# Last batch of a channel mixer: 15 block products in place of 18, the first third ahead of the batch before

## The chip, the cores and the metric

The kernel runs on one core of one Trainium2 chip. The metric is the time of one execution on the device, in microseconds (us), as the median of several runs; beside it stands a profile of one execution. TensorE (PE in the profile) multiplies matrices into PSUM, VectorE (DVE) and ScalarE (ACT) do elementwise work, GpSimd (POOL) a little at the start, and SyncE (SP) issues the DMAs. Each engine works off its own queue in order and waits for the others at semaphores.

## The reference

For 4 batches of 8 heads, 768 positions and a head size of 48, an attention with a gated outer-product state is followed by a mixer of width 8 x 48 = 384. All data are float32.

```python
f = 1.0 / (1.0 + np.exp(-f_logit))
for t in range(S):
    state = f[:, :, t, :, None] * state + np.einsum('bhd,bhe->bhde', k[:, :, t], v[:, :, t])
    y[:, :, t] = np.einsum('bhd,bhde->bhe', q[:, :, t], state)
x = np.ascontiguousarray(y.transpose(0, 2, 1, 3)).reshape(B, S, H * D)

xt = x.transpose(0, 2, 1)
h = xt @ U @ V                       # rank 32, over the positions
u = x + h.transpose(0, 2, 1)
ch = np.maximum(u @ w_ch1, 0.0) @ w_ch2      # 384 -> 1536 -> 384
return (u + ch).astype(np.float32)
```

The two big products are `u @ w_ch1` (the first layer) and the product with `w_ch2` (the second layer).

## The kernel before

`factored_path` does all the work here. Attention goes through 16 units of two heads each (4 units a batch), in chunks of 64 positions. `steps` lists a unit's pieces: `scores` (sc, L587), `kept` (pt, L608), `read` and `inner` (y, L662 and L680), `states` (ds, L624), `scan`, and of the next units `gates`, `keep`, `keys`, `read_back` and `queries`, which use VectorE's 32x32 transposes (L481) and scans (L538, L556, L645) on the tiles fz, kz, qT, X, Y, fT and added. The last piece, `inner`, copies y into the batch's x (L686, ACT).

The class `Mixer` makes the pieces of one batch's mixer. A batch has 768 positions, worked in three thirds of 256 tokens (`a` = 0, 1, 2). `before` holds `low_rank` (ph, L144), `added_up` (a second ph, L152), `mix` (pu, L169, added into x by VectorE) and per third a `turn` (put, L179): six 128x128 transposes of x on TensorE, copied to uT by ACT (L180). The first layer of a third is six pieces of `ch1` (pz, L191), each of six matmuls with 128x128 weights from w1 and 256 columns of uT. Each fills a PSUM bank, and ACT applies the relu on its way to z (L198). An f32 matmul leaves two records in the profile, each with its own weight load (PEld).

The second layer of batches 1 to 3 already uses a scheme of seven products. `sums_of` makes four sums of z on VectorE (S, held in w_raw tiles, 128x768), `quarters` has made sums of w2 beforehand, and `seven` does four steps with 12, 12, 12 and 6 matmuls of 192 columns (pw, L236), each followed by small adds on VectorE and a copy on ACT (L249). All adds of the mixer go through one helper, L159, which gives them a high priority. Steps 2 and 3 store the two output tiles. Batch 0 uses the plain second layer (po, L213).

The order on TensorE is written out by hand. `self.main` lists the first-layer pieces of a third among the second-layer steps of the one before, and `after` is the second layer of the last third. While attention works on batch b + 1, the class `Fill` deals out the mixer pieces of batch b between attention's pieces, each with a cost and when its share is due; `attention` puts out what is left at the end. Then `start_mixer` puts the pieces of `before` among those of `after`. After the last batch's attention nothing is left to go beside: its `main` and `after` stand alone, behind a check of the gates' smallest product (low, lp, lowest, ok). The order of the VectorE and ACT queues behind the first batch comes from a scheduler, by dependencies and priorities; in-order queues then keep it.

PSUM has two pools: `ps_big`, three tiles of two banks each (put, pu, sc, pt, ds, y), and `ps_mm`, two tiles of one bank (ph, pz, pw, po). A matmul that takes a tile waits until its last reader is done.

Of the kernel before, what the change touches and what calls it, by code (L numbers as in the profile page):

```python
# [10 lines left out]
F32 = mybir.dt.float32  # L11
U32 = mybir.dt.uint32
U64 = mybir.dt.uint64
I32 = mybir.dt.int32
AF = mybir.ActivationFunctionType
ALU = mybir.AluOpType
AX = mybir.AxisListType

WP = 384

RAW = 4
# [6 lines left out]

SMALLEST = struct.unpack("f", struct.pack("I", 896 << 20))[0]
LARGEST = struct.unpack("f", struct.pack("I", (1151 << 20) - 2))[0]  # L30


def weight_loader(nc, pool, dma):
# [53 lines left out]
class Fill:  # L87


    def __init__(self, pieces, portions):  # L90
        self.pieces = list(pieces)
        self.share = sum(c for c, _ in self.pieces) / portions
        self.due = 0.0
# [27 lines left out]
class Mixer:  # L121
# [2 lines left out]

    def __init__(self, tc, b, x, U, V, w1, w2, sums, ident, blocks, out, two, three, zp, ps_big, ps_mm, wide=False):
        nc = tc.nc
        P = nc.NUM_PARTITIONS
        NCH, DM = x.shape[1], x.shape[2]  # L130
        R, FF = U.shape[2], w1.shape[2]
        NG = P // R
        NDC, NFC = DM // P, FF // P
# [22 lines left out]
        def add(*args):  # L156

            with tc.high_priority(offset=AHEAD):
                nc.vector.tensor_tensor(*args)  # L159
# [25 lines left out]
        def ch1(a, j):  # L185

            pm = ps_mm.tile([P, 512], F32, name="pz", tag="mm")
            for i in range(2):
                for m in range(NDC):
                    o = (2 * j + i) * P  # L190
                    nc.tensor.matmul(pm[:, i * 2 * P : (i + 1) * 2 * P], lhsT=w1[:, m, o : o + P],  # L191
                                     rhs=uT[a][:, m, :], start=(m == 0), stop=(m == NDC - 1))
            c, k = divmod(2 * j, NI)
            if k == 0:

                own = wide and c == 1
                z[a, c] = zp.tile([P, NI, 2 * P], F32, name="zw" if own else "z")
            nc.scalar.activation(z[a, c][:, k : k + 2, :].rearrange("p i t -> p (i t)"), pm, AF.Relu)  # L198

        def store(t, o):  # L200
            nc.sync.dma_start(out=out[b, t * P : (t + 1) * P, :], in_=o)
# [18 lines left out]
        def part(a, r, c):  # L220
            return z[a, c][:, :, r * P : (r + 1) * P]

        def sums_of(a):
            for i in range(1, 5):
                s = two.tile([P, WP], U64, name="w_raw", bufs=RAW)
                S[i] = s.bitcast(F32).rearrange("p (i t) -> p i t", t=P)
            add(S[1], part(a, 1, 0), part(a, 1, 1), ALU.add)
            add(S[2], S[1], part(a, 0, 0), ALU.subtract)
            add(S[3], part(a, 0, 0), part(a, 1, 0), ALU.subtract)
            add(S[4], part(a, 0, 1), S[2], ALU.subtract)  # L230

        def products(a, *of):
            pm = ps_mm.tile([P, 512], F32, name="pw", tag="mm")
            for n, (lhs, rhs) in enumerate(of):
                for i in range(NI):
                    nc.tensor.matmul(pm[:, n * HM : (n + 1) * HM], lhsT=lhs[:, i, :], rhs=rhs[:, i, :],  # L236
                                     start=(i == 0), stop=(i == NI - 1))
            return pm
# [4 lines left out]
        def seven(a, step):  # L243
            x0, x1 = x[:, 2 * a, :], x[:, 2 * a + 1, :]
            if step == 0:
                pm = products(a, (part(a, 0, 0), w2[:, 0:NI, lo]), (part(a, 0, 1), w2[:, NI:NFC, lo]))
                s = W["s"] = two.tile([P, WP], U32, name="w_y").bitcast(F32)
                o = W["o0"] = three.tile([P, DM], F32, name="o")
                nc.scalar.copy(s[:, hi], pm[:, lo])  # L249
                add(s[:, lo], x0[:, lo], pm[:, lo], ALU.add)  # L250
                add(o[:, lo], s[:, lo], pm[:, hi], ALU.add)
            elif step == 1:
                pm = products(a, (S[2], sums[2]), (S[3], sums[3]))
                s, o = W["s"], W["o0"]
                add(s[:, hi], s[:, hi], pm[:, lo], ALU.add)
                add(o[:, hi], s[:, hi], pm[:, hi], ALU.add)
                o1 = W["o1"] = three.tile([P, DM], F32, name="o")
                add(o1.rearrange("p (n d) -> p n d", n=2), x1.rearrange("p (n d) -> p n d", n=2),
                    o[:, hi].unsqueeze(1).broadcast_to((P, 2, HM)), ALU.add)
                add(s[:, hi], s[:, hi], x0[:, hi], ALU.add)  # L260
            elif step == 2:
                pm = products(a, (part(a, 1, 1), sums[4]), (S[1], sums[1]))
                add(W["o1"], W["o1"], pm[:, 0:DM], ALU.add)
                store(2 * a + 1, W["o1"])
                add(W["s"][:, hi], W["s"][:, hi], pm[:, hi], ALU.add)
            else:
                pm = products(a, (S[4], w2[:, NI:NFC, hi]))
                add(W["o0"][:, hi], W["s"][:, hi], pm[:, lo], ALU.add)
                store(2 * a, W["o0"])

        def second(a):
            if sums is None:
# [21 lines left out]
            self.main += ready(a) + ahead[: NI // 2] + second(a) + ahead[NI // 2 :]  # L294
        self.main += ready(NA - 1)
        self.after = second(NA - 1)


def quarters(nc, pool, w2):
# [22 lines left out]
def factored_path(ctx, tc, q, k, v, f_logit, moe_U, moe_V, moe_w_ch1, moe_w_ch2, out, ok):  # L322
# [22 lines left out]

    TURNED = HP + HP // 2

    assert S % (2 * P) == 0 and H % 2 == 0 and NB < D <= PAD and PAD == 2 * NB and S % NB == 0 and W == NBL * 2 * PAD
    assert DM % P == 0 and FF % P == 0 and FF % WP == 0 and DM == WP and DM <= 512 and R % 32 == 0 and P % R == 0 and P // R <= NBL and NFC % 4 == 0 and NBL == 6
    assert NBL * PAD <= 512 and C == PAD  # L350
# [8 lines left out]

    raw = [{nm: const.tile([P, W], F32, name=f"{nm}_raw{i}") for nm in "fkq"} for i in range(2)]
    nat = [
        {nm: t.rearrange("p (c h d) -> p c h d", h=2, d=PAD) for nm, t in slot.items()}
        for slot in raw
# [54 lines left out]
    for s in range(2):  # L420
        half = causal[s * C : (s + 1) * C, :]
        nc.gpsimd.affine_select(out=half, in_=half, compare_op=ALU.is_ge, fill=0.0, base=0,
                                pattern=[[1, C]], channel_multiplier=-1)
    ends = const.tile([P, S], F32, name="ends")
    nc.vector.memset(ends, 0.0)
    nc.vector.memset(ends.rearrange("p (c t) -> p c t", t=C)[:, :, C - 1], 1.0)
    starts = const.tile([P, S], F32, name="starts")
    nc.gpsimd.memset(starts, 0.0)

    fz = [const.tile([P, S + 1], F32, name=f"fz{i}") for i in range(2)]  # L430
# [56 lines left out]
    def prepare(n):  # L487
# [33 lines left out]
        def gates():  # L521
            f0 = T["f0"] = two.tile([P, NCH], F32, name="f0")
            if n < TURNED:
                pt = on_tensor("f")
                nc.scalar.activation(halves(f)[:, :, :, 1:C], pt[:, :, :, 1:C], AF.Sigmoid)
                nc.scalar.activation(f0.rearrange("p (a c) -> p a c", a=2), pt[:, :, :, 0], AF.Sigmoid)
                follow("f")
                return
            fT = one.tile([P, S], F32, name="fT")
            turned(fT, r["f"])  # L530
            follow("f")
            fv = fT.rearrange("p (c t) -> p c t", t=C)
            nc.scalar.activation(by_chunk[:, :, 1:C], fv[:, :, 1:C], AF.Sigmoid)  # L533
            nc.scalar.activation(f0, fv[:, :, 0], AF.Sigmoid)

        def keep():
            X = T["X"] = one.tile([P, S], F32, name="X")
            nc.vector.tensor_tensor_scan(  # L538
                backwards(X, S - 1, S), backwards(f, S, S), backwards(ends, S - 1, S), 0.0,
                ALU.mult, ALU.add,  # L540
            )
            X0 = X.rearrange("p (c t) -> p c t", t=C)[:, :, 0]
            nc.scalar.copy(least[:, n, :], X0)
            X1 = two.tile([P, NCH], F32, name="X1")
            nc.vector.tensor_single_scalar(X1, X0, LEAST, ALU.max)
            nc.vector.reciprocal(starts.rearrange("p (c t) -> p c t", t=C)[:, :, 0], X1)
            whole = wholes[n % 2]
            nc.vector.tensor_tensor(whole[:, 1:NCH], T["f0"][:, 1:NCH], X0[:, 1:NCH], ALU.mult)
# [3 lines left out]
            follow("k")  # L552

        def read():
            Y = T["Y"] = one.tile([P, S], F32, name="Y")
            nc.vector.tensor_tensor_scan(Y, f[:, 0:S], starts, 0.0, ALU.mult, ALU.add)  # L556

        def queries():
# [5 lines left out]
    x_tiles = {}  # L564

    def mixer(b):
        return Mixer(tc, b, x_tiles[b], U, V, w1, w2, sums if b else None, ident, blocks, out, two, three, zp, ps_big, ps_mm, b == 0)

    def attend(n):

# [150 lines left out]
            if n + 2 < NU:  # L721
                load(n + 2, "v")

    def attention(pieces, portions, todo):

        fill = Fill(todo, portions)
        for piece in pieces:
            fill()
            piece()
        fill.rest()  # L730

    def start_mixer(b, after):

# [69 lines left out]
            f()  # L803
    for b in range(2, B):
        todo, after = m.main, m.after
        attention(steps(b * HP + 1, (b + 1) * HP + 1), 10 * HP, todo)
        m = start_mixer(b, after)
    todo, after = m.main, m.after

    low = one.tile([P, 1], F32, name="low")  # L810
# [338 lines left out]
```

## Time and profile before

| what | us |
|---|---|
| median of 9 runs | 500.92 (499.68 to 501.49) |
| the profiled execution's own time | 500.32 |
| its span, first to last instruction | 498.6 |
| TensorE matmuls busy | 483.1 |
| VectorE busy | 278.4 |
| ScalarE busy | 157.7 |
| first layer's matmuls (L191), all batches | 196.0 |
| second layer by seven products (L236), all its groups | 131.6 |
| last `inner` of attention ends | 363.6 |
| last batch's transposes (put) | 403.3 to 405.3 |
| last batch's first and second layer | 405.4 to 493.0 |

A line of the costliest groups or of the table by shape gives the line of the kernel, engine, operation, output and inputs, shapes and count, then the busy time and the mean of one in ns, then the idle time in front of it. A line of the timeline gives the start, the time from the first to the last of a run of equal instructions, and what they are. Matmuls are pipelined, so the duration of one record is longer than the spacing of two. The chain of waits follows the end back from what released what, and gives for each piece the start and the time it adds.

### The profile page before, as it was taken

What the parts mean: (1) busy time and instruction counts of PE and PEld (TensorE: products, weight loads), DVE (VectorE), ACT (ScalarE), POOL (GpSimd) and SP (SyncE); (2) the same over time, 40 slices, a digit from 0 to 9 for tenths busy, and PEclk for the clock granted to TensorE, in tenths of its full rate; (3) what the DMA queues carried; (4) which work ended last, traced back from release to release, by engine and by line L of the source; (5) the groups of instructions that cost most, each with busy time, mean ns of one, the idle gap of its engine ahead of it and who ended that gap; (6) DMA issues with size and microseconds to landing.
All of it is one profiled execution on the core that took longest, in us unless ns stands there. A gap on an engine that the chain in (4) does not pass through costs nothing.

```text
span 498.6 us, 11989 instructions
## 1 busy us (share of the span) xinstructions
PE 483.1 (97%) x5279; PEld 401.6 (81%) x5279; DVE 278.4 (56%) x402; ACT 157.7 (32%) x297; POOL 36.3 (7%) x49
## 2 busy tenths in 40 slices
PE   7997999999999999999999999999999999999995
PEld 4775688886666578898898788898899888999995
DVE  4896789778998487666665436632411431122232
ACT  2434576564434123423323122313311122101010
POOL 3001345441000000000000000000000000000000
PEclk9998999999999999999999999999999999999998
DMA  9989956784777323406234100100000000000001
GB/s 146 153 180 164 285 147 156 163 139 55 113 114 123 69 41 49 63 12 115 38 49 82 24 33 1 26 1 33 3 1 34 0 35 0 1 32 1 32 2 37
DMA packets 158676, 34.30 MB, mean 69 GB/s; under 512 B 149206, under 2 KB 157078, under 8 KB 158614
## 3 DMA queue, kind: packets, MB, share of 16 engines
q1 hardware_dynamic: 158614, 33.44, 36.5%
q8 instruction: 43, 0.70, 0.6%
q14 instruction: 19, 0.16, 0.1%
HBM read 28.70 MB, written 4.72 MB: 67 GB/s over the span
## 4 chain that ended last, share of the span: by engine, by line
PE 93%; DMA 2%; DVE 1%; issue 1%; ACT 1%; SPq 0%; DVEq 0%; ACTq 0%
PE pz L191 39%; PE pw L236 24%; PE po L213 10%; PE y L662 3%; PE y L680 3%; PE ds L624 3%; PE sc L587 3%; PE pt L504 2%; PE idle L752 2%; PE put L179 2%; PE pt L608 2%; PE ph L144 1%; PE pu L169 1%; DMA f_raw<-in_f_logit_dram 1%; DMA k_raw<-in_k_dram 1%
## 5 line engine op out<-in xcount | busy, mean ns | idle before, releaser
L191 PE MATMUL pz<-uT,w 128*128 128x256 f32 x864 | 196.0, 382 | 0.1
L191 PEld LDWEIGHTS pz<-uT,w 128*128 128x128 f32 x864 | 161.0, 190 | 22.4 <-issue 0.3
L198 ACT ACTIVATE z<-pz 128x512 f32<-128x512 f32 x63 | 37.5, 596 | 129.9 <-PE pz L191 125.8
L236 PE MATMUL pw<-w,z 128*128 128x192 f32 x324 | 56.5, 329 | 0.4 <-DVE o L159 0.4
L236 PE MATMUL pw<-zw,w_raw 128*128 128x192 f32 x324 | 55.9, 327 | 0.8 <-DVE o L159 0.8
L236 PEld LDWEIGHTS pw<-zw,w_raw 128*128 128x128 f32 x324 | 53.0, 190 | 2.2 <-DVE o L159 2.1
L236 PEld LDWEIGHTS pw<-w,z 128*128 128x128 f32 x324 | 52.8, 190 | 2.3 <-DVE o L159 1.6
L159 DVE TENSOR_TENSOR w_raw<-z 128x768 f32<-128x768 f32 x18 | 17.2, 954 | 56.3 <-ACT z L198 56.3
L538 DVE TENSOR_TENSOR_SCAN X<-fz,ends 128x768 f32<-128x768 f32 x16 | 28.1, 1756 | 9.9 <-ACT fz L533 5.1
L69 POOL TENSOR_TENSOR w<-w_y,w_r 128x384 int32<-128x384 int32 x24 | 30.2, 1257 | 36.5 <-DVE w_y L68 30.8
L556 DVE TENSOR_TENSOR_SCAN Y<-fz,starts 128x768 f32<-128x768 f32 x16 | 27.9, 1745 | 0.2
L213 PE MATMUL po<-w,zw 128*128 128x384 f32 x72 | 25.6, 499 | 0.0
L213 PE MATMUL po<-w,z 128*128 128x384 f32 x72 | 25.3, 496 | 0.0
L594 DVE TENSOR_TENSOR A<-sc,causal 128x768 f32<-128x768 f32 x16 | 15.2, 948 | 16.9 <-PE sc L587 16.9
L159 DVE TENSOR_TENSOR w_y<-x,pw 128x192 f32<-128x192 f32 x9 | 3.2, 354 | 38.2 <-ACT w_y L249 38.2
L650 ACT COPY st<-added 128x576 f32<-128x576 f32 x12 | 14.6, 1220 | 23.7 <-DVE added L645 23.7
L159 DVE TENSOR_TENSOR w_y<-w_y,pw 128x192 f32<-128x192 f32 x18 | 6.3, 349 | 25.5 <-PE pw L236 25.5
L213 PEld LDWEIGHTS po<-w,zw 128*128 128x128 f32 x72 | 12.9, 189 | 8.7 <-issue 1.2
L213 PEld LDWEIGHTS po<-w,z 128*128 128x128 f32 x72 | 13.1, 190 | 8.5 <-DVE o L159 0.6
L680 PEld LDWEIGHTS y<-v_nat,A 64*64 64x64 f32 x768 | 13.5, 139 | 7.7 <-issue 6.3
L236 PE MATMUL pw<-w,w_raw 128*128 128x192 f32 x108 | 19.2, 328 | 0.0
L66 DVE TENSOR_SCALAR w_y<-w_y 128x384 f32<-128x384 f32 (+3 forms) x27 | 11.8, 438 | 12.3 <-ACT w_y L64 12.1
(101 smaller groups left out, 531.9 us busy)
## 6 DMA issues: line engine op xcount, KB each, us to landing
w_raw<-in_moe_w_ch_dram SPq DMA_DIRECT2D x18, 384.0 KB, 3.9
out_dram<-o SPq DMA_DIRECT2D x24, 192.0 KB, 1.9
v_nat<-in_v_dram SPq DMA_DIRECT2D x16, 144.0 KB, 3.0
v_nat<-in_v_dram SPq DMA_DIRECT2D x32, 72.0 KB, 2.9
zw<-in_moe_w_ch_dram SPq DMA_DIRECT2D x6, 384.0 KB, 5.6
f_raw<-in_f_logit_dram SPq DMA_DIRECT2D x20, 96.0 KB, 3.1
k_raw<-in_k_dram SPq DMA_DIRECT2D x20, 96.0 KB, 2.6
q_raw<-in_q_dram SPq DMA_DIRECT2D x20, 96.0 KB, 2.7
```

Source lines behind the costliest of these rows:

```text
L69: nc.gpsimd.tensor_tensor(dst.bitcast(I32), shaped(y.bitcast(I32)), shaped(r), ALU.add)
L159: nc.vector.tensor_tensor(*args)
L191: nc.tensor.matmul(pm[:, i * 2 * P : (i + 1) * 2 * P], lhsT=w1[:, m, o : o + P], rhs=uT[a][:, m, :], start=(m == 0), stop=(m == NDC - 1))
L198: nc.scalar.activation(z[a, c][:, k : k + 2, :].rearrange("p i t -> p (i t)"), pm, AF.Relu)
L213: nc.tensor.matmul(pm, lhsT=z[a, i // NI][:, i % NI, s * P : (s + 1) * P], rhs=w2[:, i, :], start=(i == 0), stop=(i == NFC - 1))
L236: nc.tensor.matmul(pm[:, n * HM : (n + 1) * HM], lhsT=lhs[:, i, :], rhs=rhs[:, i, :], start=(i == 0), stop=(i == NI - 1))
L538: nc.vector.tensor_tensor_scan(backwards(X, S - 1, S), backwards(f, S, S), backwards(ends, S - 1, S), 0.0, ALU.mult, ALU.add,)
L556: nc.vector.tensor_tensor_scan(Y, f[:, 0:S], starts, 0.0, ALU.mult, ALU.add)
L587: nc.tensor.matmul(sc[part[s ^ par], par, c * C : (c + 1) * C], lhsT=T["k"][rows[par], chunk[2 * c + s]], rhs=T["q"][rows[par], chunk[2 * ...
L594: nc.vector.tensor_tensor(T["A"], sc[:, :, 0 : NBL * C].rearrange("p h (c i) -> p h c i", i=C), causal.unsqueeze(1).unsqueeze(1).broadcast ...
L624: nc.tensor.matmul(ds[par * PAD : (par + 1) * PAD, s, c * D : (c + 1) * D], lhsT=T["kb"][part[s ^ par], par, i, :], rhs=vt[part[s ^ par], ...
L680: nc.tensor.matmul(o(s, par, c), lhsT=T["A"][part[s ^ par], par, c, :], rhs=vt[part[s ^ par], c, par, :], start=False, stop=True, skip_gro ...
```

## The change

The first layer of the last batch is done by another scheme. A third of 256 tokens times w1 is a product of a 2 x 3 grid of blocks (128 tokens x 128 channels) with a 3 x 3 grid (128 channels x 512). Plainly that is 18 products of blocks. The scheme takes 15 products, of sums of blocks of x (`X_SUMS`, 10 sums of 128x128 a third) with sums of blocks of w1 (`W_SUMS`, 14 sums of 128x512, made once). The results (`VALUES`) are put together from the products: per third two copies on ACT and 19 sums of 128x512 on VectorE, then six relus on ACT, in place in z.

A product is four matmuls of 128x128 weights and 128 columns, with the block of w1 as weights. Two products share a tile of `ps_big` (`two_of`), so a third has eight pieces (seven pairs and a single one), and the sums follow as soon as their products are there.

The order changes too. In the last attention round, what `Fill` has not dealt out is kept back. `sum_of_w` is called beside the pieces of the second half of that round. Then the last batch's `low_rank`, `added_up` and `mix` come first, each followed by one of the kept pieces; the transposes and two rounds of sums of x follow; and the first third's pieces (`early`) are put among the rest of batch 2's mixer. The check of the gates comes after that, then thirds 1 and 2, each among the second-layer steps of the third before.

Room is found in tiles that are free by then. The raw f, k and q of one slot, ends, X, Y and fT become parts of one tile `late`, the other slot and starts parts of `other`, and z becomes `z_all`. The sums of w1 go over `late`, fz and added, the sums of x over v_nat and st, the values over kz, A and qT, z of thirds 0 and 2 over `other`, and the four sums S of third 1 over blocks of w1 that no product uses any more. The products of the last third's second layer take a tile of `ps_big`.

```diff
+X_SUMS = (
+    (7, 3, '+', 5), (6, 2, '+', 5), (11, 3, '+', 6), (13, 0, '+', 11), (8, 4, '-', 6), (9, 1, '+', 8),
+    (10, 2, '+', 8), (12, 9, '-', 0), (15, 10, '-', 12), (14, 3, '-', 12),
+)
...
+PRODUCTS = (
+    ((2, 17),), ((7, 18),), ((11, 20),), ((6, 21),), ((13, 0),), ((1, 3),), ((8, 15),), ((4, 19),),
+    ((9, 10),), ((10, 16),), ((3, 22),), ((12, 11),), ((0, 12),), ((15, 13),), ((14, 9),),
+)
+VALUES = (
+    (13, 'p0', None, None), (15, 'p1', None, None), (14, 'v15', '+', 'p2'), (12, 'v14', '-', 'p3'), (6, 'p4', '-', 'v14'),
+    (0, 'v6', '-', 'v13'), (0, 'v0', '+', 'p5'), (11, 'v12', '+', 'v13'), (11, 'p6', '-', 'v11'), (3, 'p7', '-', 'v11'),
...
         def products(a, *of):
-            pm = ps_mm.tile([P, 512], F32, name="pw", tag="mm")
+            if room and a == NA - 1:
+                pm = ps_big.tile([P, 2, 512], F32, name="pw", tag="big")[:, 0]
+            else:
+                pm = ps_mm.tile([P, 512], F32, name="pw", tag="mm")
...
+            def settle():
+                while todo:
+                    n, p, sign, q = todo[0]
+                    if any(o is not None and got(o) is None for o in (p, q)):
+                        return
...
+                    if q is None:
+                        nc.scalar.copy(dst, left)
+                    else:
+                        combine(dst, left, sign, right)
...
+                    if n < 6 and not any(v[0] == n for v in todo):
+                        nc.scalar.activation(dst, dst, AF.Relu, scale=float(SIGNS[n]))
+
+            def two_of(k):
+                pm = ps_big.tile([P, 2, 512], F32, name="pp", tag="big")
+                for i, of in enumerate(PRODUCTS[k : k + 2]):
+                    for r in range(FG):
+                        for xn, wn in of:
+                            nc.tensor.matmul(
+                                pm[:, i, r * P : (r + 1) * P], lhsT=room["w"](wn)[:, r * P : (r + 1) * P],
+                                rhs=x_node(a, xn), start=((xn, wn) == of[0]), stop=((xn, wn) == of[-1]),
+                            )
+                    have[k + i] = pm[:, i, 0 : FG * P].rearrange("p (i t) -> p i t", t=P)
+                settle()
...
+        if room:
...
+            i = len(self.before) - NA + 1
+            self.before[i:i] = more(0)
+            self.before[i + 2 : i + 2] = more(1)
+            self.early = fewer(0)
+            self.main = []
+            for a in range(NA - 1):
+                f, s = fewer(a + 1), second(a)
+                self.main += ready(a) + f[:4] + (more(a + 2) if a == 0 else []) + f[4:5]
+                if a < NA - 2:
+                    self.main += s[:1] + f[5:6] + s[1:2] + f[6:7] + s[2:3] + f[7:] + s[3:]
+                else:
+                    self.main += f[5:6] + s[:1] + f[6:] + s[1:2] + ready(NA - 1) + s[2:]
...
         todo, after = m.main, m.after
-        attention(steps(b * HP + 1, (b + 1) * HP + 1), 10 * HP, todo)
-        m = start_mixer(b, after)
+        pieces = steps(b * HP + 1, (b + 1) * HP + 1)
+        if b == B - 1:
+            pieces = beside(pieces, 10 * (HP - 2), [lambda i=i: sum_of_w(i) for i in range(len(W_SUMS))])
+        rest = attention(pieces, 10 * HP, todo, b < B - 1)
+        if b < B - 1:
+            m = start_mixer(b, after)
+
+    m, rest = mixer(B - 1), rest + after
+    pieces = [p for pair in zip(m.before[:3], rest) for p in pair] + m.before[3:]
+    rest = rest[3:]
+    for i, piece in enumerate(m.early):
+        n = -(-len(rest) // (len(m.early) - i))
+        pieces += [piece] + rest[:n]
+        rest = rest[n:]
+    for _, piece in pieces:
+        piece()
     todo, after = m.main, m.after
```

## The prediction

> **What bounds the kernel now.** I read the busy times first, then the chain that ended last, then the stretches around the change, then single instructions.
>
> The page says that TensorE's matmuls are busy almost always, and VectorE (DVE) about half the time:
>
> ```profile
> PE 483.1 (97%) x5279; PEld 401.6 (81%) x5279; DVE 278.4 (56%) x402; ACT 157.7 (32%) x297; POOL 36.3 (7%) x49
> ```
>
> The chain of waits from the last attention matmul to the end, in order of time (start, us, what), is matmuls with almost no holes:
>
> ```profile
> 363.00 0.64 PE y L680 x44
> 363.64 13.85 PE pw L236 x84
> ...
> 385.26 3.90 PE pw L236 x24
> 389.16 1.41 PE ph L144 x12
> ...
> 403.31 1.97 PE put L179 x18
> 405.27 0.11 PE lp L813
> 405.38 23.31 PE pz L191 x108
> 428.69 13.65 PE pw L236 x84
> 442.35 15.54 PE pz L191 x72
> ```
>
> So in this part a microsecond off TensorE is a microsecond off the kernel, as long as nothing else becomes late. The busy times of three stretches (columns: stretch, length, then busy time per engine) tell how much room VectorE has:
>
> ```profile
> 320.00:340.00 20.00, 20.00 (x268) 18.77 (x268) 9.15 (x15) 4.83 (x8) 0.00 (x0) 1.00 0.05 14
> 340.00:363.60 23.60, 23.60 (x457) 19.59 (x449) 6.91 (x8) 7.75 (x13) 0.00 (x0) 1.00 0.03 11
> 405.10:493.00 87.90, 87.86 (x471) 81.97 (x468) 21.20 (x41) 12.81 (x23) 0.00 (x0) 1.00 0.04 12
> ```
>
> In the last 88 us VectorE works 21 us. The granted clock is 1.00 in all three.
>
> **Part 1: fewer products on TensorE.** Each f32 matmul leaves two records. From the chain: 128x256 takes 23.31 / 108 = 0.2158 us a record (L191), 128x192 takes 13.65 / 84 = 0.1625 (L236). The slope between them is 0.0533 / 64 = 0.833 ns a column, so 128 columns should take 0.1625 - 64 x 0.000833 = 0.109 us, if the weight load does not become the limit. That is the one unknown that decides the sign: the new matmuls have half the columns, and each still loads its own 128x128 weights. Transposes of 128 columns do run at 1.97 / 18 = 0.109, but their weight loads last 140 ns in the table by shape, those of f32 matmuls 190 ns, so they prove nothing alone. The nearest case is a 128-column instruction followed by an f32 matmul with a full weight load. The timeline has one at 405 us:
>
> ```profile
> 405.11 0.27 PE L813 MATMUL lp<-ident,low 128*1 128x128 f32 x1
> 405.11 3.97 PEld L191 LDWEIGHTS pz<-uT,w 128*128 128x128 f32 x19
> 405.22 4.05 PE L191 MATMUL pz<-uT,w 128*128 128x256 f32 x18
> ```
>
> The load starts with the matmul before it (405.11) and the matmul that needs it starts at 405.22. The 190 ns of a load are thus mostly latency: the array may go on about 110 ns after its start. The single records show ten such steps (six L504 to L191, three L179 to L191, and this one), all 109 to 110 ns from start to start. Load and columns just balance.
>
> Here a rule speaks against the change. The Trainium skill, "TensorE: Matmul & The Clock Gate", section "Back-to-back issue gap", says that in a real stream of loads and matmuls with 128 columns the spacing is about 81 ns where the columns alone would take 56, so 25 ns of each load stay visible. By the row a record costs 0.109, by the rule (an estimate from that page) 0.109 + 0.025 = 0.134. I take the row: it has this kernel's f32 loads, and ten cases agree within 1 ns.
>
> A third of the last batch (256 tokens) has 36 x 2 = 72 records of 0.2158 = 15.54 us before. Now it has 15 products x 4 matmuls x 2 = 120 records of 0.109 = 13.10. Saved: 2.44 a third, 7.3 us in all. By the rule it would be 16.1 a third, 1.6 us lost in all.
>
> **Part 2: sums on VectorE and copies on ScalarE (ACT).** No row is 128x512, so I interpolate between L159's 128x384 (0.55 us) and 128x768 (0.95): 0.683. For 128x128, from 0.35 at 192 and 0.55 at 384: 0.285. A third now needs 19 value sums (13.0), 10 sums of x (2.85), and as before four sums of z (3.8) and the small adds of seven() (3.6): 23.2 us of VectorE against 13.10 + 13.65 = 26.75 of TensorE. It fits, at 87%; ACT gets two copies and six relus of 0.6 instead of six relus.
>
> In-order queues make the order matter. With T the end of a third's last product, TensorE does the last step of seven() (1.95) and four pairs of products (1.75 each); the fifth pair, at T + 8.9, needs the PSUM tile of the second. VectorE's queue meanwhile holds the last value sum (0.7 with its wait), waits for the relu (0.6), then has the four z sums with a small add among them (4.2) and only then the two sums that free that tile (1.4): T + 7.2, or T + 7.6 where the ok flag's two operations stand between. Margin 1.3 to 1.7 us. In the middle of a third the next pair comes after a 3.9 us seven() step and the margins are larger. At the end, the z sums of third 2 are done at about T + 7, under three steps of seven() that last 9.75, then step 0 (3.9) that needs only z. So 0 on the path, but this cover is the thinnest of the plan.
>
> The first third runs beside the rest of batch 2. There only two of the three wide PSUM tiles turn: the third transpose's tile waits for its copy, ACT has that copy behind the relus of two pz pieces, and its destination is free only after the third pz piece. VectorE starts with 20 sums of x (5.7 us). But every early pair is followed by a pz or seven() step of 2 to 4 us, and following the queues pair by pair I find VectorE done 1.4 us or more ahead of each need. 0 taken, 0 to 2 for the range.
>
> **Part 3: sums of weights in the last attention round.** 14 x 0.683 = 9.6 us more on VectorE, one about 255 us, the others between 300 and 358, where the stretches leave it over half its time. Between them stand attention's scans and transposes, whose results TensorE takes many us later. The tightest is a group of four (2.7 us) ahead of the adds that free a PSUM tile at 338.7: they end at about 340.65, and pz wants the tile at 340.63. Cost 0.2, at most 1.
>
> **Part 4: the order after attention.** Before, 25 us of products (L236, L191) separated the last y from ph. Now ph follows y at once and waits for the copy of y into x, which the timeline has at 363.71 for 0.64: idle until 364.4, +0.76. Next, the second ph (0.65 us of columns) is followed by a seven() step whose PSUM tile waits for the copy of that ph into h:
>
> ```profile
> 394.51 0.81 PE L152 MATMUL ph<-h,blocks 128*128 128x384 f32 x2
> 395.35 0.48 ACT L154 COPY h<-ph 128x384 f32<-128x384 f32 x1 [4.25 <-PE ph L152]
> 395.50 2.22 PE L236 MATMUL pw<-w,z 128*128 128x192 f32 x12 [0.19 <-DVE o L159]
> ```
>
> The columns end at 395.16; with the copy ending at 395.83 the next matmul starts at about 395.88: +0.72, in place of the 0.34 lost there today. The two pu adds into x, the output stores on SP (nothing urgent is queued behind them, all loads are issued) and the flag's chain keep their cover of a 3.9 us step. POOL gets only memsets of other tiles at the start.
>
> **The sum.** -7.3 + 0.76 + 0.72 - 0.34 + 0.2 = -6.0 us. The profiled execution took 500.32 us with a span of 498.6; it becomes 494.4 with a span of 492.6. The median shown is 500.92, 0.6 above that execution: 494.9, rounded up to 495.0.
>
> **Rivals.**
> (a) *Weight loads bind, slower.* If a 128-column f32 record in a long stream costs more than the single steps show, 360 records carry it. The other terms cost 1.3 us, so the change breaks even at 6.0 / 360 = 17 ns above 0.109, at 0.126 us. At the rule's 0.134 it is 9.0 us worse than my sum: 504.0. For it: no stream of such records is in the trace. Against: the ten steps of 109 to 110. Chance 0.08.
> (b) *VectorE becomes the bound.* If a value sum, with one operand in PSUM, costs over 0.683 + 3.55 / 19 = 0.87 us, a third is set by VectorE. At 0.95 a third is 28.3 against 26.75, and with waits at both ends some 5 us of the gain go: 500. For it: 87% load and in-order queues. Against: L594 reads PSUM at 0.948 for 768 elements, no slower than sums from SBUF. Chance 0.07; around no change, both signs.
> (c) *Late buffers.* The chain is as I think, but one or two margins of 1.3 to 1.7 us are wrong and each third loses about 1 us: 497 to 498.5. Chance 0.13.
> (d) *The weight sums disturb attention* by more than 1 us, for example through a wait of the one that overwrites the scan's tile until ACT has copied it: 496.5 to 498. Chance 0.07.
> (e) That the change doesn't do what it says is excluded: 45 products of four 128x128 matmuls stand in the built program where 18 pieces of six 128x256 stood.
>
> **How the numbers follow.** My sum has 0.65, with its own range 494.0 to 496.5. Below it little can be gained: only the two waits of part 4. Cases (c) and (d) reach to 498.5, (b) to 500 and (a) to 504; leaving out (a), half of (b) and a bit at the low end gives 493.8 to 498.9. A measurement of this kernel tells about 0.2%, 1 us, from no change. Faster by more: 0.65 + 0.13 + 0.07 + a third of (b) = 0.87. Within 0.2%: 0.03. Slower: (a) and the rest of (b), 0.10.
>
> **What would show it.** Part 1: the new group's matmuls at 0.109 us spacing, each third's 120 records in 13.1 us wherever they run unbroken; 0.126 or more makes the prediction wrong. Part 2: VectorE busy some 48 us more (3 x 15.9) from the end of attention on, TensorE's idle time before the new products close to 0; waits of them on DVE of over 1 us in all would be (b) or (c). Part 3: attention's last y ends within 0.5 us of 363.6. Part 4: two holes of about 0.7 us at ph and the step after it.

## The result, and the profile after

The changed kernel takes 495.06 us (median of 10 runs, 493.84 to 496.46), against 500.39 for the kernel before on the same chip (31 runs). The ratio is 0.9894 with a 95% interval of 0.9874 to 0.9914: 5.3 us faster. The forecast was 495.0, with a span of 492.6 us in the profiled execution. That span is 492.5, and the time of that execution 494.24.

The page's busy times of the changed kernel:

```profile
PE 474.3 (96%) x5423; PEld 400.2 (81%) x5423; DVE 329.0 (67%) x503; ACT 161.4 (33%) x303; POOL 36.4 (7%) x49
```

TensorE has 144 records more and is busy 8.8 us less. VectorE has 101 more and is busy two thirds of the span.

The chain of waits of the changed kernel, from the last attention matmul to the end (start, us, what):

```profile
362.21 0.89 PE y L850 x48
363.10 0.02 issue
363.12 0.65 ACT x L856
363.77 0.04 issue
363.82 1.48 PE ph L172 x12
365.30 4.10 PE pw L273 x24
369.40 0.66 PE ph L180 x2
370.08 0.49 ACT h L182
370.57 0.04 issue
370.61 4.17 PE pw L273 x24
...
419.21 8.93 PE pp L370 x80
428.14 3.90 PE pw L273 x24
...
446.26 10.72 PE pp L370 x96
...
463.56 23.42 PE pw L273 x144
```

Two holes are in it, where an ACT piece stands between matmuls: ahead of the first ph, and ahead of the step after the second ph. Past them there is nothing but matmuls: no new product waits for a sum. The stream of products (pp) takes 8.93 / 80 = 0.1116 and 10.72 / 96 = 0.1117 us a record, where the forecast had 0.109.

The busy times of the changed kernel in the stretches that were shown of before (the last one ends earlier now):

```profile
320.00:340.00 20.00, 20.00 (x268) 18.68 (x261) 13.57 (x22) 4.30 (x8) 0.00 (x0) 1.00 0.01 2
340.00:363.60 23.60, 23.06 (x413) 19.03 (x412) 7.64 (x9) 8.13 (x14) 0.00 (x0) 1.00 0.06 20
405.10:487.00 81.90, 81.86 (x592) 81.49 (x590) 55.03 (x102) 13.30 (x24) 0.00 (x0) 1.00 0.05 18
446.30:456.90 10.60, 10.60 (x97) 10.60 (x96) 10.10 (x16) 2.34 (x4) 0.00 (x0) 1.00 0.06 20
```

In the third line VectorE works 55.0 of 81.9 us. That is an average: in the last line, which covers the longest unbroken run of products, it works 10.1 of 10.6 us. The weight loads (PEld) are now as full as the matmuls: 81.49 us of 81.90, where they had 81.97 of 87.90.

**Where the time went.** I compare stretches between two events of one execution, since the start of the program scatters: the first ph of batch 1, which comes long before the work that was changed, starts at 163.51 us before, at 162.89 after, and between 161.8 and 164.3 in the executions below. From there to the end of the last y it takes 200.13 us before and 200.17 after. From the last y to the last matmul it takes 129.31 before and 123.91 after. So the change gives 5.40 us, all of it behind attention. The other 0.7 us between the two spans (498.6 and 492.5) are 0.6 us of a start that happened to be early and 0.1 us behind the last matmul.

### The profile page after: what moved, and what is told of

Same layout as the page of the kernel before. It is cut to its first block, busy times and chain, and to the rows that moved or that the text cites. A ratio compares the mean times of both kernels' runs of the same rounds, so it can differ in the third digit from the quotient of the medians.

```text
span 492.5 us, 12410 instructions
## 1 busy us (share of the span) xinstructions
PE 474.3 (96%) x5423; PEld 400.2 (81%) x5423; DVE 329.0 (67%) x503; ACT 161.4 (33%) x303; POOL 36.4 (7%) x49
## 4 chain that ended last, share of the span: by engine, by line
PE 90%; DMA 3%; SPq 2%; DVE 1%; ACT 1%; issue 1%; POOL 0%; DVEq 0%; ACTq 0%
PE pz L219 28%; PE pw L273 25%; PE po L244 10%; PE pp L370 8%; PE y L832 3%; PE sc L757 3%; PE y L850 3%; PE ds L794 2%; PE pt L633 2%; PE pt L778 1%; SPq L521 1%; DMA zw<-in_moe_w_ch_dram 1%; PE put L207 1%; DMA late<-in_f_logit_dram 1%; PE idle L934 1%; PE pu L197 1%
## 5 line engine op out<-in xcount | busy, mean ns | idle before, releaser
L219 PE MATMUL pz<-uT,w 128*128 128x256 f32 x648 | 149.3, 383 | 1.1 <-ACT uT L208 1.1
L219 PEld LDWEIGHTS pz<-uT,w 128*128 128x128 f32 x648 | 119.9, 190 | 17.9 <-issue 1.0
L229 ACT ACTIVATE z_all<-pz 128x512 f32<-128x512 f32 x45 | 26.8, 595 | 63.2 <-PE pz L219 63.1
L273 PE MATMUL pw<-w,z_all 128*128 128x192 f32 x252 | 44.2, 330 | 0.2 <-DVE o L187 0.2
L273 PEld LDWEIGHTS pw<-w,z_all 128*128 128x128 f32 x252 | 40.7, 190 | 2.4 <-DVE o L187 1.3
L667 DVE TENSOR_TENSOR_SCAN late<-fz,late 128x768 f32<-128x768 f32 x16 | 28.1, 1756 | 10.0 <-ACT fz L662 5.1
L685 DVE TENSOR_TENSOR_SCAN late<-fz,other 128x768 f32<-128x768 f32 x16 | 27.9, 1746 | 0.1
L244 PE MATMUL po<-w,z_all 128*128 128x384 f32 x72 | 25.3, 496 | 0.0
L244 PEld LDWEIGHTS po<-w,z_all 128*128 128x128 f32 x72 | 13.1, 190 | 8.5 <-DVE o L187 0.6
L370 PE MATMUL pp<-v_nat,late 128*128 128x128 f32 x144 | 18.5, 275 | 0.0
```

The source lines that it names most:

```text
L244: nc.tensor.matmul(pm, lhsT=z[a, i // NI][:, i % NI, s * P : (s + 1) * P], rhs=w2[:, i, :], start=(i == 0), stop=(i == NFC - 1))
L370: nc.tensor.matmul(pm[:, i, r * P : (r + 1) * P], lhsT=room["w"](wn)[:, r * P : (r + 1) * P], rhs=x_node(a, xn), start=((xn, wn) == of[0]) ...
L667: nc.vector.tensor_tensor_scan(backwards(X, S - 1, S), backwards(f, S, S), backwards(ends, S - 1, S), 0.0, ALU.mult, ALU.add,)
```

## Experiments

The expectations rest on the trace of after. The 15-product scheme, the new order and VectorE's slack each get runs of their own. "The last stretch" is the time from the last y to the last matmul in the profiled execution, 123.91 us in the changed kernel.

### The base

Twice the changed kernel ran again, once in each later group of runs.

> The changed kernel itself once more, as the base of the runs beside it: 495.1 us, within 0.5.

> The changed kernel once more, on the same chip as the two beside it: 494.6 to 495.1 us, 123.9 us from the last y of attention to the last matmul.

Measured: 494.64 us (492.88 to 496.24) and 494.40 us (493.73 to 495.75), ratios to before 0.9894 (0.9866 to 0.9922) and 0.9885 (0.9851 to 0.9918). The last stretch is 123.91 in both. The second median is 0.2 us below what was expected. Single executions scatter by 2 to 3 us, the stretch does not (123.91 in three executions): effects under 1 us are read from it.

### The order without the scheme

The pieces stand in the new order, but the first layer is the old one: 18 products with 256 columns, and no sums but those of z. The cut shows the main edits. In the rest, the four sums of third 1 go back to the usual tiles, and those of third 2 come after third 1's last two steps and not ahead of them; the order of the matmuls is the new one.

```diff
             z[a, 0], z[a, 1] = zf[:, 0:NI, :], zf[:, NI:, :]
+            return first(a)
...
             def more(a):
-                return [(1, lambda: sums_of_x(a))] if a < NA else []
+                return []
...
-            pieces = beside(pieces, 10 * (HP - 2), [lambda i=i: sum_of_w(i) for i in range(len(W_SUMS))])
+            pieces = beside(pieces, 10 * (HP - 2), [])
```

> The new order of the pieces (first third of the last batch ahead, beside the rest of batch 2) with the old first layer: 18 products in matmuls of 256 columns, no sums of x, of weights or of values. Theory (the order alone costs its two holes, and all of the gain is of the fewer products): about 1 us slower than before, span 499.5 to 500, time near 501.3, ratio to before 1.000 to 1.003. Rival (the order itself brings part of the gain): 495 to 498.

Measured: 501.98 us, ratio 1.0029 (1.0010 to 1.0048), span 500.1, last stretch 131.47, which is 2.16 more than before. The order alone makes the kernel slower, by more than the 1 us that I gave it. Besides the two holes it has a third, which the changed kernel doesn't have. The timeline of this kernel at the boundary of the first two thirds:

```profile
419.90 0.96 DVE L187 TENSOR_TENSOR w_raw<-other 128x768 f32<-128x768 f32 x1 [2.40 <-ACT other L229]
420.90 0.96 DVE L187 TENSOR_TENSOR w_raw<-w_raw,other 128x768 f32<-128x768 f32 x1
421.02 0.27 PE L1008 MATMUL lp<-ident,low 128*1 128x128 f32 x1
421.77 0.35 DVE L187 TENSOR_TENSOR o<-w_y,pw 128x192 f32<-128x192 f32 x1
422.04 0.95 DVE L187 TENSOR_TENSOR w_raw<-other 128x768 f32<-128x768 f32 x1
422.17 0.51 PEld L219 LDWEIGHTS pz<-uT,w 128*128 128x128 f32 x3 [1.23 <-DVE o L187]
422.18 0.70 PE L219 MATMUL pz<-uT,w 128*128 128x256 f32 x2 [0.88 <-DVE o L187]
```

The next pz piece wants a one-bank tile that the last step of `seven` has filled. Its add (o<-w_y,pw) is queued on VectorE behind two z sums of 0.96 us, so TensorE stands still: 1.15 us from the start of lp to the start of pz, where 0.11 would do, so 1.04 lost. The new pairs take two-bank tiles from the other pool and pass this queue by. That the scheme spares a wait that the new order would otherwise have is part of its worth, and the forecast didn't have it as a term.

### The scheme with 18 products

Three products per third get a second term. Everything else (order, tiles, sums, copies) is the changed kernel's.

```diff
-    ((2, 17),), ((7, 18),), ((11, 20),), ((6, 21),), ((13, 0),), ((1, 3),), ((8, 15),), ((4, 19),),
-    ((9, 10),), ((10, 16),), ((3, 22),), ((12, 11),), ((0, 12),), ((15, 13),), ((14, 9),),
+    ((2, 17),), ((7, 18),), ((11, 20), (11, 17)), ((6, 21),), ((13, 0),), ((1, 3),), ((8, 15),), ((4, 19),),
+    ((9, 10), (9, 18)), ((10, 16),), ((3, 22),), ((12, 11),), ((0, 12), (0, 20)), ((15, 13),), ((14, 9),),
```

> Three of the 15 products of each third get a second term, so that TensorE issues 18 block products per third with all sums, copies and the order of the changed kernel kept (72 records more in all; the values computed are no longer the reference's). Theory (the gain is TensorE's records and nothing else): 72 x 0.1116 = +8.0 us on the changed kernel, about 503. So 18 products with this order, in matmuls of 128 columns, are slower than the 18 of before. Rival (the gain is of the new order, or VectorE sets the thirds and TensorE has slack): +0 to +3 us, 495 to 498.

Measured: 503.47 us, ratio 1.0052 (1.0033 to 1.0071), last stretch 131.95: +8.04 on the changed kernel, 72 records at 0.1117. TensorE has no slack where these records were added, three places in each third: together they cost what their spacing says.

With this the 5.40 us come apart in three steps of the last stretch:

| step | last stretch, us | difference |
|---|---|---|
| before | 129.31 | |
| the new order, old products | 131.47 | +2.16 |
| 18 products in 128 columns, with all sums | 131.95 | +0.48 |
| 15 products | 123.91 | -8.04 |

The middle step is small because two things work against each other: 432 records at 0.1117 in place of 216 at 0.2158 cost 1.6 us more, and the hole of 1.04 at lp goes away. The two make +0.6 where +0.48 was measured; the rest is not assigned.

### Half the columns

Each new matmul is cut in two of 64 columns, with the same weights.

```diff
-                            nc.tensor.matmul(
-                                pm[:, i, r * P : (r + 1) * P], lhsT=room["w"](wn)[:, r * P : (r + 1) * P],
-                                rhs=x_node(a, xn), start=((xn, wn) == of[0]), stop=((xn, wn) == of[-1]),
-                            )
+                            for o in (0, P // 2):
+                                nc.tensor.matmul(
+                                    pm[:, i, r * P + o : r * P + o + P // 2], lhsT=room["w"](wn)[:, r * P : (r + 1) * P],
+                                    rhs=x_node(a, xn)[:, o : o + P // 2], start=((xn, wn) == of[0]), stop=((xn, wn) == of[-1]),
+                                )
```

> Each new matmul of 128 columns is cut into two of 64 columns with the same weights: as many columns, twice the records (360 more in all). Theory (the weight load, not the columns, sets the 111.6 ns of a record): a record stays near 0.11 us, so 360 x 0.11 = +40 us, about 535. Rival (the columns set it, and the load hides): a record of 64 columns takes about half, 0.056 us, and the time stays within 2 us of the changed kernel, 495 to 497. Between: the spacing measured at 64 columns is the floor that a load sets.

Measured: 534.63 us, ratio 1.068 (1.064 to 1.072), last stretch 164.11: +40.2, 360 records at 0.1117. The chain of this kernel has the first six pairs of third 2, which took 10.72 us in 96 records, now as many columns in 192 records:

```profile
472.56 21.38 PE pp L371 x192
```

21.38 / 192 = 0.1114 us: a record of half the columns costs the same. The rival (the columns set the price) is out. A fixed price of every record is out too: the last 48 records of attention (y, 48 columns, with loads of 64 rows and columns) take 0.89 us in the chain of the changed kernel, 0.019 each. What the records at 64 and at 128 columns share is the load of 128x128 weights.

### VectorE's slack

One z sum of each third is done twice, then all four.

```diff
             add(S[a, 4], part(a, 0, 1), S[a, 2], ALU.subtract)
+            if room:
+                add(S[a, 4], part(a, 0, 1), S[a, 2], ALU.subtract)
```

```diff
             add(S[a, 4], part(a, 0, 1), S[a, 2], ALU.subtract)
+            if room:
+                add(S[a, 1], part(a, 1, 0), part(a, 1, 1), ALU.add)
+                add(S[a, 2], S[a, 1], part(a, 0, 0), ALU.subtract)
+                add(S[a, 3], part(a, 0, 0), part(a, 1, 0), ALU.subtract)
+                add(S[a, 4], part(a, 0, 1), S[a, 2], ALU.subtract)
```

> In each third of the last batch one of the four z sums of 128x768 is done a second time, 0.87 us more of VectorE a third, 2.6 in all. Theory (VectorE has slack: the sum that frees the second pair's PSUM tile ends 1.9 us before the fifth pair wants it): nothing moves, 0 with at most 0.3 us either way. Rival (VectorE already sets the thirds): +2.6 us, 497.7.

> All four z sums of each third are done twice, 3.5 us more of VectorE a third, 10.5 in all. Theory (the slack is 1.9 us at the fifth pair of thirds 1 and 2): each of the two fifth pairs waits 3.5 - 1.9 = 1.6 us, and nothing else is late: about +3 us, 498. Rivals: the slack is wider than that, 0; VectorE sets the thirds, +10.5, 505.6.

The slack that these texts speak of, in the timeline of the changed kernel at third 1's fifth pair (st,late x16 is the fifth pair, the sum ending at 424.30 is the second of the two that free its tile):

```profile
423.61 0.69 DVE L187 TENSOR_TENSOR qT<-A,pp 128x512 f32<-128x512 f32 x1
...
426.19 1.95 PE L370 MATMUL pp<-st,late 128*128 128x128 f32 x16
```

Measured, one z sum more: 495.35 us, ratio 0.9915 (0.9881 to 0.9948), 0.7 above the changed kernel beside it, but the intervals of the two ratios overlap; last stretch 124.09, so +0.18 for 2.6 us more of VectorE. All of it is lost at one place, the sixth pair of third 2. The changed kernel has this there (the sum is the one that frees the pair's tile):

```profile
453.44 0.69 DVE L187 TENSOR_TENSOR other<-other,pp 128x512 f32<-128x512 f32 x1
...
455.03 1.06 PE L370 MATMUL pp<-uT,added 128*128 128x128 f32 x8
```

The sum ends at 454.13, 0.90 us ahead of the pair, half of the slack at the fifth pair (1.9). With one z sum more it ends at 455.41 and the pair starts at 455.55, late by just that much.

Measured, four more: 498.21 us, ratio 0.9963 (0.9945 to 0.9982), 3.6 above the changed kernel beside it, where I had 3. The first wait comes where I had it. The same place in the timeline of the kernel with four more:

```profile
427.78 0.68 DVE L187 TENSOR_TENSOR qT<-A,pp 128x512 f32<-128x512 f32 x1
...
428.61 2.02 PE L375 MATMUL pp<-st,late 128*128 128x128 f32 x16 [0.86 <-DVE qT L187]
```

The sum ends at 428.46 and the fifth pair starts at 428.61, 1.02 us late by the spacing of the records. In third 2 the wait is not so much at the fifth pair (0.27 late) as at the sixth (2.01 late), where the slack was half as wide; two of the doubled sums also fall between the value sums ahead of it:

```profile
459.86 1.91 PE L375 MATMUL pp<-uT,added 128*128 128x128 f32 x8 [1.84 <-DVE other L187]
```

Together 3.3 us of waits. So VectorE does not set the thirds of the changed kernel, but it is near: ahead of the fifth pair some 2 us of work are free, ahead of the sixth pair of third 2 less than the 0.87 us of one sum, and what goes beyond is paid on TensorE.

### The weight sums

The 14 sums are left out, and blocks of w1 stand in for them.

```diff
     def w_node(n):
         if n < 9:
             return w1[:, n // 3, n % 3 * FG : (n % 3 + 1) * FG]
-        return w_places[W_PLACES[n - 9]]
+        return w_node(n % 9)
...
-            pieces = beside(pieces, 10 * (HP - 2), [lambda i=i: sum_of_w(i) for i in range(len(W_SUMS))])
+            pieces = beside(pieces, 10 * (HP - 2), [])
```

> The 14 weight sums in the last attention round are left out, and plain blocks of w1 stand in for them in the products (so the first layer of the last batch is not the reference's). Theory (they lie beside other work and cost about 0.1 us): -0.1, at most -0.3; the end of attention comes at the same time after the first low-rank product of batch 1. Rival (they disturb attention): -1 us or more.

Measured: 497.01 us, ratio 0.9940 (0.9914 to 0.9967), slower than with the sums. From batch 1's ph to the last y it took 200.14 us, against 200.17 with the sums, so nothing moved in attention. The last stretch was 128.35, 4.44 longer, and the timeline of this kernel says why:

```profile
444.57 0.96 DVE L187 TENSOR_TENSOR w<-z_all 128x768 f32<-128x768 f32 x1 [0.70 <-ACT z_all L363]
...
447.68 2.03 PE L370 MATMUL pp<-uT,w 128*128 128x128 f32 x8 [2.58 <-DVE w L187]
```

I had made the wait myself: z sums of third 1 are written over blocks of w1 (w<-z_all), and my stand-ins made products of third 2 read those blocks. The second try stands in only blocks 0 and 3, which the changed kernel also reads in plain form.

```diff
-        return w_node(n % 9)
+        return w_node((0, 3)[n % 2])
```

> The weight sums left out again, but only the two blocks of w1 that the changed kernel itself still reads in plain form stand in for them, so that no block is read whose place third 1's z sums overwrite (the first layer of the last batch is not the reference's). Theory (the sums lie beside other work): the 2.6 us hole ahead of third 2's first pair is gone, 123.9 us from the last y to the last matmul, and 0 to 0.2 us off the changed kernel's median. Rival (the sums cost something after all): 0.5 us or more below it.

Measured: 494.49 us, ratio 0.9887 (0.9853 to 0.9921), beside 494.40 for the changed kernel. The last stretch is 123.91 and attention 200.13. The 9.6 us of VectorE in the last attention round cost 0.04 us.

### One kept piece ahead of ph

The kept step of batch 2 that came after the first ph now comes ahead of it, and the others move up by one.

```diff
-    pieces = [p for pair in zip(m.before[:3], rest) for p in pair] + m.before[3:]
-    rest = rest[3:]
+    pieces = rest[:1] + [p for pair in zip(m.before[:3], rest[1:]) for p in pair] + m.before[3:]
+    rest = rest[4:]
```

> One kept piece of work (a product step of batch 2) is put between the end of attention and the last mixer's first low-rank product, so that copies run beside TensorE's work. Theory (in this stretch every microsecond of TensorE counts, and the two holes of 0.76 and 0.57 us are the price of the new order): both holes shrink to about 0.35 us in all, which the order had in the kernel before. Span about 491.6 us, 0.9 below the changed kernel's 492.5; time about 494.2. Rival (the holes are paid elsewhere, by VectorE being late in the first third, where one product step fewer lies between the new pairs): no gain, or 0 to 1 us slower than the changed kernel.

> The kernel with one kept piece ahead of the first low-rank product again, now beside the changed kernel on one chip. Theory: 122.9 us from the last y to the last matmul, as in its first run, and a median 1.0 us below that of the changed kernel. Rival (the difference seen is the start-up's scatter between executions): medians within 0.3 us.

Measured: 493.88 us, ratio 0.9858 (0.9831 to 0.9885), and 492.81 us, ratio 0.9867 (0.9829 to 0.9905). The last stretch is 122.90 both times, 1.01 below the changed kernel. The timeline of the first run:

```profile
363.43 4.17 PE L273 MATMUL pw<-w,z_all 128*128 128x192 f32 x24
367.53 1.49 PE L172 MATMUL ph<-x,U 128*32 128x384 f32 x12
368.94 4.17 PE L273 MATMUL pw<-zw,w_raw 128*128 128x192 f32 x24
372.94 0.81 PE L180 MATMUL ph<-h,blocks 128*128 128x384 f32 x2
373.94 2.22 PE L273 MATMUL pw<-w,z_all 128*128 128x192 f32 x12 [0.19 <-DVE o L187]
```

ph comes in without a wait, as the copy of y into x lies beside the 4.1 us of pw. After the second ph 0.35 us are left (372.94 + 0.65 to 373.94), as before the change. Nothing else became late. In medians the gain is less sharp. On the one chip where both ran it is 1.6 us (492.81 against 494.40), where I had 1.0. Over all chips it is 0.6: 493.84 over the 12 executions of both runs, 494.44 over the 12 of the two bases; the intervals of the ratios overlap, and the stretch decides. By the stretch this is the fastest version of those run.

## Why the prediction was right, point by point

**What bounds the kernel: right.** Every record added to the thirds (eighteen products, half the columns) came out at its full 0.1117 us, and filling the holes gave back 1.01 of their 1.21 us.

**Part 1, fewer products: right in sign, mis-sized by 0.9 us.** The term was 360 records at 0.109. Measured are 0.1116 to 0.1117, so 13.4 us a third, 2.14 saved, 6.4 in all and not 7.3. The step that was off is "load and columns just balance", read from single steps. The new matmuls stand in 13 unbroken runs. At the head of each run one step, from the start of a record to the start of the next, is spared: the step into the run where the record ahead of it has 128 columns too (109 ns, two runs, behind a transpose and behind lp), otherwise the first step within the run (109 to 110 ns, eleven runs). Every later step takes 111 to 112. With 64 columns the first step within takes 55 to 59 ns in all 13 runs, and every later one again 111 to 112. So a step at the head shows the columns alone, and the price of load behind load shows only past it. The ten steps that the forecast rested on were all steps into a run, so they could not show it. That the loads and not the columns set the period is seen from the half columns: 21.38 / 192 = 0.1114 for half the work per record. Why the head is spared is not shown. Columns show through where they are the longer of the two, as in the 0.1625 of 192 columns.

Between the row and the rule that was weighed against it, the row was nearer. The Trainium skill, "TensorE: Matmul & The Clock Gate", section "Back-to-back issue gap", puts 25 ns of the load on top of 128 columns (81 against 56). Here, with f32 loads, 2.6 ns are on top of the 109 of the columns. Rival (a), which breaks even at 17 ns, is out, but what it named is the one term that fell short.

**Part 2, VectorE: right.** VectorE's busy time behind attention went from 34.3 to 76.0 us, 41.7 more; I had 48. A sum of 128x512 has a record of 0.68 us as interpolated, but in a row the next starts 0.60 after the last, so records overlap. That fits the margin at the fifth pair, 1.9 us in thirds 1 and 2 (424.30 to 426.19 in third 1) and not 1.3 to 1.7. Zero was right on the path: no product waits. But the reading of the order had two slips that happened to cost nothing. In the middle of a third the next pair was to come after a step of `seven`; in third 2 the sixth pair follows the fifth at once, and there the margin is 0.90, less than any that the forecast named. And in the first third the fourth and fifth pair stand together (32 records at 397.41 in the full chain), with no step between. Rivals (b) and (c) are out: 2.6 us more of VectorE cost 0.18.

**Part 3, the weight sums: right, and smaller.** 0.04 us where I took 0.2. Rival (d) is out.

**Part 4, the order: right.** By the spacing of record starts: from the last y to the next matmul it takes 0.977 us with ph next and 0.148 with a product step next, so the first hole costs 0.83 (forecast 0.76). From the last record of the second ph to the next step it takes 1.054, against 0.675 before: 0.38 (forecast 0.72 - 0.34 = 0.38). Together 1.21 in place of 1.14. Moving one piece gave 1.01 back. What the forecast lacked is that the old products would have had a third hole of 1.04 in this order. It didn't have to be in the sum, as the new products don't meet it, but the order by itself is dearer than the sum's terms for it.

**The sum.** 6.4 less, 1.2 and 0.04 more make -5.2. The last stretch and attention show -5.36 together; the other 0.2 I can't assign. The forecast had -6.0, and still met the span to 0.1 us because that execution started 0.6 us early: that closeness is luck. So is the median's, 495.06 for 495.0: the gain was 0.6 smaller than forecast, but the kernel before came out at 500.39, 0.5 below the 500.92 that the forecast started from. The medians agree with the stretch: 494.64 against 500.18 and 494.40 against 499.90, 5.5 us each.

## What to carry to other kernels

A scheme with fewer products pays only by the records that it takes away at their real price in a stream, and smaller blocks raise that price: at 64 and at 128 columns an f32 record cost the same here, so between 64 and 128 the columns are free and records are not. Take the price from a run of equal instructions, not from single steps where the kind changes. When a piece is moved to the front, put something that is ready ahead of its first wait; and count the queue of the engine that frees the tiles, where a small add behind two large ones held up TensorE. And check each place where one piece follows another at once: the thinnest margin seen here was at one that the forecast had missed.

## What the runs showed of the hardware

**A stop of 2 us can cost nearly as much again.** In two profiled executions TensorE stood still for 2.0 and 2.7 us in the middle of a full stretch. Both then worked off the next 16 records at half speed, in 3.4 and 3.5 us. The granted clock is the column ahead of the last two. First the kernel that left the weight sums out and made itself a wait:

```profile
444.29:447.70 3.41, 0.83 (x7) 0.57 (x5) 3.09 (x5) 0.25 (x1) 0.00 (x0) 1.00 0.16 59
447.70:451.12 3.42, 3.42 (x16) 3.42 (x17) 0.83 (x1) 0.00 (x0) 0.00 (x0) 0.50 0.00 0
451.12:454.53 3.41, 3.41 (x33) 3.41 (x33) 1.27 (x2) 1.07 (x2) 0.00 (x0) 1.00 0.02 7
```

Then the kernel with all z sums doubled:

```profile
456.60:460.01 3.41, 1.57 (x14) 1.40 (x13) 3.41 (x7) 0.26 (x1) 0.00 (x0) 1.00 0.00 0
460.01:463.42 3.41, 3.41 (x17) 3.41 (x18) 2.79 (x5) 0.97 (x2) 0.00 (x0) 0.50 0.00 0
```

In the first kernel the records come every 0.213 us, then every 0.1116 again: 16 of them take 3.49 us in place of 1.79. These 1.7 us and 2.74 of the stop make the 4.44 by which that stretch was longer. In the second, 16 records take 3.41, and the half clock makes about 1.7 of the 5.14 by which the last stretch of its profiled execution (500.85 us, the slowest of its ten) was longer. Stops of 0.57 to 1.04 us, at ph, at lp and at the fifth pair, left the clock at 1.00.

The half clock lasts 3.41 us both times, and the changes of the clock fit a grid of that length: before it fell, it had stood at 1.00 for 436.91 us in one trace and 406.19 in the other, 128 and 119 times 3.413. In the stretch of 3.41 us just ahead of the fall TensorE worked 0.83 and 1.57 of 3.41 us; around the stop of 1.04 it worked 2.54 of such a stretch, and the clock stayed. So where a stop lies against the grid may count as much as its length. That was not tried, but it would fit the medians: they are only 2.4 and 3.6 us above the changed kernel beside them, less than 4.44 and 5.14. How many of the other executions had the half clock is not on record.

The Trainium skill, "TensorE: Matmul & The Clock Gate", section "What's actually happening", has the half clock and its 3.4 us, and gives an idle window of about 3.4 us as what brings it on; here stops of 2.0 and 2.7 us were enough. For the forecast this means that rival (b) may have been priced too low: a stop of that length could have cost nearly double.

**The weight load has a period of its own.** A load's record lasts 192 ns, and one follows another every 111.6 ns, whether the matmul between them has 64 or 128 columns. Sharing one load between two thirds' columns (256 at a time, 0.2158 for both) would save 7 ns a pair of records by these figures, an estimate; that wasn't tried.
